# The causal triangle of an attention layer as zeros written after the exponential, in place of mask products

## The chip, the cores and the metric

The kernel runs on one core of one Trainium2 chip. The metric is device time in microseconds (us) of that core. PE is TensorE, DVE is VectorE, ACT is ScalarE, POOL is GpSimd, SP is the engine that here only issues DMAs.

## The reference

The computation is two rounds of a layer A and a layer B, each added to a residual `x` of 2048 tokens and width 512, with 32 heads of width 16. Layer A is a causal attention inside each of four segments of 512 tokens, mixed with a running memory:

```python
mask = (ar[:, None] < ar[None, :]) * -1000000000.0
for s in range(N):                       # N = 4 segments of L = 512
    logits = einsum('bhqd,bhkd->bhqk', qs, ks) * scale + mask
    p = softmax(logits)
    a_dot = einsum('bhqk,bhkd->bhqd', p, vs)
    ...                                  # a_mem from the memory M, z
    o = g * a_mem + (1.0 - g) * a_dot
    M = M + phi(ks)^T vs ; z = z + sum(phi(ks))
x = x + o @ wo
```

Layer B is a linear attention. Its keys pass through `softmax(pk)` and `softmax(-pk)` over the 16 features of a head, so each head and token needs the sum of 16 exponentials, twice:

```python
phi_k = concat([softmax(pk), softmax(-pk)])
kv = einsum('bhsf,bhsd->bhfd', phi_k, v) ; z = phi_k.sum(over tokens)
o = (phi_q @ kv) / (phi_q @ z + 1e-06)
x = x + o @ wo
```

## The kernel before, in words

Tokens lie in 16 tiles of 128; a segment is four of them. For each of the two rounds L the program goes through the four segments s: normalise, project to keys and queries per group g of eight heads (`a_proj`), attention in two halves i0 = 0 and 2 of the segment (`a_att`), the output projection, and then the keys of layer B for that segment (`b_keys`). After the fourth segment come the queries of layer B (`b_query`), and in round 0 the normalisation and projections for round 1 run among them.

**Attention.** TensorE is used as two row groups of 64 rows, so matmuls come in pairs that run side by side. In `a_proj`, VectorE makes four masked copies of the keys per group with `tensor_scalar` (label Km, L679, tile pQ, 128 in all), so that heads can be stacked along the contraction. In `a_att` the logits of a key tile wholly before the queries are one group of products (label S) and one exponential into a tile PT. For the diagonal there are two kinds of tile: PF (pool pF, three buffers, label Sf, twice for each group of each half, 128 in all, 896 columns exponentiated) and PE (pool pE, two buffers, label Sd, once, 64 in all, 768 columns). Both add the causal mask on TensorE, as a last pair of products `two` times `tri`, where `tri` holds -1e9 above the diagonal of a 64 by 64 block and `two` stacks two unit matrices: 128 columns for Sf and 256 for Sd. So the exponential on ScalarE (L351, a helper) already writes zeros in the triangle. The products P·V (label PV, L326 through another helper) then take P as weights and read PF, PE and PT directly from ScalarE.

**Layer B's keys.** For a pair of token tiles, ScalarE writes exp(k) and exp(-k), 1024 columns each; VectorE reduces each with one `tensor_reduce` over 16 features (label Zred, L945, 28 of 1024 columns and 8 of 512), then takes reciprocals (rZ) and scales the values (Vt).

**Other VectorE work that the prediction names.** xn normalises (L594, L598, 64 instructions), phmax and phadd (L634, L635, 48 each) build phi, nmul and nadd (L1043, L1049) are in `b_query`, oadd (L851) adds the memory's part to the attention, Kev, Qev, Vev and res are evacuations of TensorE's results that ScalarE or VectorE may do. GpSimd computes the reciprocal root of the normalisation (rstd, L585 and L587, 60 each), scales one weight matrix in setup (L530, four instructions) and clears buffers.

**What sets the order.** Each operation is entered in a graph with the engines that may run it, a planner's cost in ns for each, and a flag `port` on operations that the planner is told use a shared resource of VectorE and GpSimd. The planner itself is not in the program: its answer is a compressed table (`ORDER`) that `place` reads: a global order of all operations, the engine of each, and the buffer of each tile. `emit` turns that into one in-order list of instructions for each engine, with a semaphore wait wherever an operation needs another engine's result or a buffer that another still uses. An engine never passes an instruction that waits.

Of the kernel before, what the change touches and what calls it, by code (L numbers as in the profile page):

```python
# [16 lines left out]
D = 512  # L17
# [280 lines left out]
class Kernel:  # L298
# [97 lines left out]
    def alloc(self):  # L396
# [9 lines left out]
        self.two64 = sb("two64", [128, 2, 64], BF16)  # L406
        self.tri = sb("tri", [128, 64], BF16)
# [42 lines left out]
    def setup(self):  # L450
# [39 lines left out]
        for g in range(NG):  # L490
            for hf in range(2):
# [16 lines left out]
        v(lambda e: e.tensor_tensor(self.two64[:], self.ident[:, 0:64][:, None, :].to_broadcast([128, 2, 64]),  # L508
                                    self.ident[:, 64:128][:, None, :].to_broadcast([128, 2, 64]), ALU.add), 120, [R("ident")], [R("two64")])
        tw = self.T(self.p1, "fold")  # L510
        v(lambda e: e.memset(tw.t[:, 0:128], -1e9), 150, [], [tw], eng=P)
        v(lambda e: e.affine_select(tw.t[:, 0:128], tw.t[:, 0:128], [[-1, 128]], ALU.is_gt, 0.0, base=0, channel_multiplier=1), 250, [tw], [tw], eng=P)
        for hf in range(2):
            v(lambda e, hf=hf: e.tensor_copy(self.tri[64 * hf:64 * hf + 64, :], tw.t[64 * hf:64 * hf + 64, 64 * hf:64 * hf + 64]), 100,
              [tw], [R("tri", hf)])
# [142 lines left out]
    def a_proj(self, L, s):  # L658
# [7 lines left out]
        for g in range(NG):  # L666
# [11 lines left out]
            for sl in range(4):  # L678
                fn = lambda e, KM=KM, KT=KT, sl=sl: e.tensor_scalar(  # L679
                    KM.t[:, :, sl % 2, :, 64 * (sl // 2):64 * (sl // 2) + 64], KT.t[:].rearrange("p (j h k) -> p j h k", j=4, h=2),  # L680
                    self.m4[:, sl:sl + 1], None, op0=ALU.mult)
                self.g.op({"dve": (262.0, fn)}, [KT, R("m4")], [KM[sl]], label="Km", port=True)
# [85 lines left out]
    def a_att(self, L, s, i0):  # L768
# [7 lines left out]
        oT = self.oT[("a", L, s * 4 + i0)] = self.T(self.p2, "oT")  # L776
        two = lambda hf: self.two64[64 * hf:64 * hf + 64].rearrange("p a b -> p (a b)")
        tri = lambda hf, n: self.tri[64 * hf:64 * hf + 64, None, :].to_broadcast([64, n, 64])
        trir = [R("two64"), R("tri", 0), R("tri", 1)]
        for gg in range(2):  # L780
            PV = self.T(self.pD, "pv")
            for g in (2 * gg, 2 * gg + 1):
# [5 lines left out]
                for j in range(i0 + 1):  # L788
                    for p in range(2):
# [6 lines left out]
                        else:  # L796
                            P = PF[p] = self.T(self.pF, "PF")
                            self.mm(lambda S=S, j=j, p=p, key=key, qry=qry: [
                                (S.t[:, hf * 512 + 256 - 192 * x:hf * 512 + 512 - 256 * x], key(hf, j, p, x), qry(hf, 64 * x, 256 - 64 * x), x == 0, False)
                                for x in range(2) for hf in range(2)] + [  # L800
                                (S.t[:, hf * 512 + 64:hf * 512 + 448].rearrange("p (b c) -> p b c", b=2)[:, :, 0:64], two(hf), tri(hf, 2), False, True) for hf in range(2)],
                                [], rd + trir, [S], opens=[P], label="Sf", rows=64, dur=252)
# [4 lines left out]
                self.mm(lambda S=S, key=key, qry=qry: [  # L807
                    (S.t[:, hf * 512 + p * 192 + 64 * (1 - x):hf * 512 + p * 192 + 192 - 128 * x], key(hf, i0 + 1, p, x), qry(hf, 128 + 64 * x, 128 - 64 * x), p + x == 0, False)
                    for p in range(2) for x in range(2) for hf in range(2)] + [
                    (S.t[:, hf * 512:hf * 512 + 384].rearrange("p (a b) -> p a b", a=2)[:, :, 0:128], two(hf), tri(hf, 4), False, True) for hf in range(2)],  # L810
                    [], rd + trir, [S], opens=[PE], label="Sd", rows=64, dur=286)
# [110 lines left out]
    def b_keys(self, L, c, parts):  # L922
# [4 lines left out]
        for part in parts:  # L927
            Es, Vts = {}, {}
            units = [part[i:i + 2] for i in range(0, len(part), 2)]
            for u in units:  # L930
# [9 lines left out]
                for sgn in range(2):  # L940
# [3 lines left out]
                             ACT.Exp, 512 * n, [S[0], S[512]][:n], [E[sgn]], scale=1.0 - 2.0 * sgn, label="kexp")  # L944
                    fn = lambda e, sgn=sgn, eo=eo, Z=Z, n=n: e.tensor_reduce(Z.t[:, 0:64 * n].rearrange("p (k s h) -> p k s h", k=n, s=2)[:, :, sgn, :],  # L945
# [177 lines left out]
COPIED = {(L, t) for L in range(2) for t in range(16)}  # L1123
N_WARM = 26
# [17 lines left out]
yRioR}L^Vpezz889_oz(@EPZ{ZWTjjL%5J%#7+40h8VdWb9OJf6c&^Z+m7Dr!NUsU^LJ4)g|6;1hg`X)rs!h2)qCCtxa^hy^hUcBJLBf@;!QYDKl^DXpW{^o-I{7wS
ssC=1o5^fU@HP(x}&S*a)Wpk~yLn$rt-Oi$<~bffmPp4w7(+DvUIExv+h*o!h#Z`w#3s19wRP4t}hQ(byN2WT{AqwG|V^58|<PTS}bU0{dl2sNgQY!Xh!DL4kl;to1
WTWKjBqvtpdGtn~2NH6dpy~F`@hz8OrdPv9V1ofkn^oU;JM?6hu=q!E0yx4%oV>&#+reb^?LH(&54WcGAk_OXNDo<nR8jYo<RFx{wI2umna0m^h@>q?kQw1DF<LNRD
qwhGH&eKGiKtJ#bT_8rE@e5X>ulO4K&>MV<?{E@Lri%C;r_gIEOmC?Oy`gu61XPNOQfbOTFX<KKq*lB&|429K1HC7rT$G<~Q32{pQ>i|kqX_s7Kj1XFPB-W_O{Y7Qm
vWP!e3XX@5~mqdh-Ok7-j;u&KKwpCpuW5m_T#1T9;N2}c^ZC~2JtdDpFYzUl9ZVb=2>`Jt|&Wi$J6l~+){g<m1pA)`KSghpyE`9zS1lzOS5SqEh0l@QPUh+Os7~9o|
FgDY4(kl&^eZgXXJC~Jex<kc}kv(=iwdrcS^;(@tiz8&%itKPP{ws%#-mSG=dkS5)?ocsS4%gl_?)j&b#oDd;sst2Xe-Ps3ZYT!GlTh5DMVKcpx9ngLnw<$$Rl0yf<
IQm-A2>!iVxOw2H6hV|jT#ijU?M_#{4=kKqM*C=W--!;<EP6Sti6aXddC&%;w;9)Sw+BD^SX!OQZ9B)G#{@?yLkk3`e>bRL;X@XEY6FU`yFGb{?7WixmcUW%{dCHWL
ykyqj~`FcK;2lJ}D8n4d7@mV}P-@xbb*?c3P&%^RCJR*<4CvYE^ya2DkBk?(WE|1Kk@MwGsU&vSRMSKCT$=C2&d?jDYm++;0D__hfi_Lr!pCV%Ms60BK$ZPXDyb<5V
8}seFF5khM@TR;Tug{zDojf+5Dt7T{qB-BqgTxWOhsWSCc>~^%$K`SOUcQg-=fUDAPsoq)1N<P5#}n~$JU&0qLqw>!#t-r1`~*MAPw~V&0YA;p@U#2^zr+vo@a!VL%  # L1150
&+jP+!1g2E&h(*=I{9(evg0T*SSwT;?u=r9v}k66Fx(H<wxZ=K2yvR-}zmBlYinj_<jC>KjcsOGyZ{p;h#AZKlm~Eia+PC`3s&(zTq$Vad|?5kRr82p+q{FUZ#<0Wd
=z?2raA#E5e9yBD{zoA_^{yh$JG5C?cwuBj$;CVz!toGRpa4fruvJi|8Vz$Rabz%rdJ?CSr+&Vv$%ZmWUW4fru><ifl5wOfKSx)MBYvCenx;GLeWYa?0f*g~%n-irn
&`+$y$-wc?OmC$@_nV!cQyc8PQ%mDnu~%RKUkOe`wOBqF`YAXbQsqLN%GPRmpBj4UHh%Dgg@C?e0wvhtiPDtC%KVz1aB_KBn-v&b!0i7X<ISS_-Oyds+@EV7FtqO>?
K^NFIOm?$Iii?X7exFCy*0wRaFD9eiy;*zW&_KW=TfG8jjikzaLC?raXHDaU4B`S*7a<C{RDv8SCnyez;$jkDIye@}`s-m74Dr$*M;<4N;p2&Rif+#4ji^}q%xGIau
LbAB5DXNQVqPD0Zs>n;?vbZA3$t|M1EUb#C`eKk8tQv?CvaoC@hKb^8xM(Gsi4v-$9HK^up{l4Vrb@}%@{YVAPKq0{kvJvlh^FF@Xf95Ro8pYPC928_vaV<>&WhXOs
%Rqah{NKXI3kXUr?RwcEhecpVzR0xr>JSFx@;@DiB4jwny&83xALYuCXS01qNAuGM~RW*nz$>vi?XVRD5r+0xU!;(Cx@$^Vvx8e-^upkytpM#i2E|W>>&Dx=CZfwEZ
T{FqLLb*2C9;(vMQy@sPd|`s-i}zx1xfos%EHaYP6cE=BamLzN)TjsQ%);Xd!=yE~1xsCclclVuTv0V#!(Ri(oRg9HVBdvFd@`sUFH*Dvqovzlle(fdo}cg8VGIiud
xlY$=wj6>7g)s1~R>YP>q2)~eNNu3DqksR?SLx+m(Wy6V1Yp%$w}YMg4RK8S`gp-dnLh=HP=d?_A?B?=X(M)HgND%;Br@|%1mma3=Xg>0gls+Y2!s;@rCTB^4CC>yE
93gs*LQGAlMWk=akHkQp)Yc*Q5Qq9$RHAXa4ZPZ@XK($pH)F<&sJQiccXYow5Q|(m~`CL2^L29!KmHX5dwNZ^1yVV2{Ms8AjR86%^bx;$9R$*nZYAPR!7vj4Jr^9HH
;dNNOQgOLTbySsgClyXMlhGtstz;b;T}G01WuP1<zRMU=$jGv@YAucGr8>zfI!Ic%RqasQRfrDN+mzCYWMWxeYwgG+GQ13y_2eYcS-uuRMUib}Z)Ic+?dXU)g7#^nt  # L1160
&XH4>%%Hg2kE0KKnLq1>X<sH>g!YLkZPc#=%~8B>>}IBs=B7GrjM(Ws<u9%d@_Q3Bed+ILZp<Z)fx3eZj^O&EnQe|k_B~FSwt7oMRhk>Oc&QBbRX4MS>-67>Z-b_n6
# [67 lines left out]
```

## Time and profile before

| | |
|---|---|
| median of 3 runs | 483.2 us (482.02 to 483.73) |
| span of the profiled execution | 481.9 us |
| time of that execution beside its span | not listed; the runs' median is 1.3 us above the span |
| PE busy | 452.9 us (94%), 11582 matmuls |
| DVE busy | 438.3 us (91%), 920 instructions |
| ACT busy | 425.9 us (88%), 560 instructions |
| POOL busy | 63.8 us (13%), 145 instructions |
| mean granted TensorE clock | 0.988 |

Busy time is the time that at least one instruction of the engine is running, by the records; records of neighbours on one engine overlap a little, and those of matmuls a lot. A row of the groups view reads: line, engine, operation, output<-input by the program's names, shapes, count | busy us, mean ns of one | idle us of the engine just before them, and what ended it. A row by source line or tile gives least/median/greatest ns. A row of the timeline gives start us, us, engine, line, operation, names, shapes and how many neighbouring instructions are merged. A row of the waits gives who waited for whom: us in total, times, longest us. A row of the windows gives the stretch in us, its length, then busy us and count of PE, PEld (weight loads), DVE, ACT and POOL, then the granted clock, the DMA share and GB/s.

### The profile page before, as it was taken

The page shows a single profiled execution, that of the slowest core. Times are in us where ns is not written, and L with a number is a line of the kernel's source. Part 1 is how long each engine was busy: PE and PEld are TensorE (multiplying, and loading weights), DVE is VectorE, ACT ScalarE, POOL GpSimd, SP SyncE. Part 2 cuts the span into 40 slices and gives each one's busy share as a digit, 9 for nine tenths or more (in the row PEclk, how much of TensorE's full clock was granted, in tenths as well). Part 3 has the DMA queues.
Part 4 walks back from the last instruction along what each step waited for, and adds up shares of the span by engine and source line. Part 5 has one row for each costly group of instructions (what it writes and reads, how often), then busy time and mean ns, then how long its engine had stood idle before and what let it go on. Part 6 is the DMA issues. An engine that isn't in the chain of part 4 may idle for free.

```text
span 481.9 us, 25218 instructions
## 1 busy us (share of the span) xinstructions
PE 452.9 (94%) x11582; PEld 298.4 (62%) x11582; DVE 438.3 (91%) x920; ACT 425.9 (88%) x560; POOL 63.8 (13%) x145
## 2 busy tenths in 40 slices
PE   8798889999989999998999999999999999999895
PEld 3346665757767677666555677576667666666553
DVE  4998999899889999898999999999999897998883
ACT  2598999999989998578999999999999999776892
POOL 2801120101010110200231041020002020110000
PEclk9999999999999999998999999999999999999799
DMA  8735254350144212200225344432204403100256
GB/s 216 199 83 139 39 90 69 47 86 21 41 68 69 37 15 48 41 1 5 46 52 96 57 72 59 79 67 47 31 4 62 77 16 59 37 12 3 46 93 196
DMA packets 89451, 30.37 MB, mean 63 GB/s; under 512 B 76000, under 2 KB 89344, under 8 KB 89344
## 3 DMA queue, kind: packets, MB, share of 16 engines
q1 hardware_dynamic: 88992, 28.46, 32.1%
q8 instruction: 91, 1.49, 1.3%
q10 hardware_dynamic: 288, 0.26, 0.2%
q0 software_dynamic: 64, 0.02, 0.1%
q14 instruction: 16, 0.13, 0.1%
HBM read 6.32 MB, written 2.10 MB: 17 GB/s over the span
## 4 chain that ended last, share of the span: by engine, by line
PE 54%; DVE 20%; ACT 17%; DMA 3%; issue 2%; SPq 2%; POOL 1%; DVEq 0%
PE D L341 35%; PE D L326 18%; ACT p L351 9%; ACT pF L351 5%; DVE p L635 3%; DVE pQ L679 2%; DVE stats L577 2%; ACT pE L351 2%; SPq L364 2%; DVE p L360 1%; DMA X<-in_A_x_dram 1%; DVE p L598 1%; DVE pK L360 1%; DVE p L847 1%; DMA pX<-p 1%
## 5 line engine op out<-in xcount | busy, mean ns | idle before, releaser
L351 ACT ACTIVATE p<-D 128x1024 bf16<-128x1024 f32 (+1 forms) x276 | 251.5, 956 | 27.5 <-PE D L341 15.9
L351 ACT ACTIVATE pF<-D 128x896 bf16<-128x896 f32 x128 | 117.3, 938 | 2.7 <-PE D L326 2.0
L326 PE MATMUL D<-pK,pQ 64*128 64x256 bf16 (+3 forms) x1536 | 113.9, 243 | 6.1 <-DVE pQ L679 2.3
L326 PEld LDWEIGHTS D<-pK,pQ 64*128 64x128 bf16 x1536 | 54.9, 94 | 45.6 <-ACT p L351 5.8
L326 PE MATMUL D<-pV,pF 64*128 64x34 bf16 x1024 | 75.8, 176 | 1.7 <-ACT pE L351 0.5
L326 PE MATMUL D<-pW,pF 64*128 64x34 bf16 x1024 | 73.0, 176 | 0.5 <-issue 0.5
L585 POOL TENSOR_SCALAR rstd<-mv 128x1 f32<-128x1 f32 x60 | 18.6, 321 | 357.4 <-DVE mv L578 357.4
L341 PE MATMUL D<-pX,WA_k 64*128 64x512 bf16 x256 | 64.7, 376 | 0.7 <-DVE pX L360 0.7
L341 PE MATMUL D<-pX,WA_q 64*128 64x512 bf16 x256 | 64.7, 377 | 0.1
L326 PEld LDWEIGHTS D<-pV,pF 64*128 64x128 bf16 x1024 | 56.8, 93 | 5.3 <-issue 2.2
L326 PEld LDWEIGHTS D<-pW,pF 64*128 64x128 bf16 x1024 | 52.4, 93 | 1.3 <-issue 0.5
L351 ACT ACTIVATE pE<-D 128x768 bf16<-128x768 f32 x64 | 52.5, 830 | 0.8 <-PE D L326 0.4
L326 PE MATMUL D<-pV,p 64*128 64x34 bf16 x1024 | 52.2, 175 | 0.9 <-issue 0.6
L326 PE MATMUL D<-pW,p 64*128 64x34 bf16 x1024 | 51.1, 176 | 0.0
L326 PEld LDWEIGHTS D<-pV,p 64*128 64x128 bf16 x1024 | 46.7, 93 | 2.7 <-ACT p L351 0.5
L326 PE MATMUL D<-tri,two 64*128 64x128 bf16 (+1 forms) x384 | 46.2, 234 | 0.0
L326 PEld LDWEIGHTS D<-pW,p 64*128 64x128 bf16 x1024 | 45.1, 93 | 1.6
L577 DVE BATCH_NORM_STATS2 stats<-X 128x6 f32<-128x512 bf16 x64 | 42.7, 680 | 3.7 <-DMA X<-in_A_x_dram 3.4
L326 PE MATMUL D<-pV,pE 64*128 64x34 bf16 x512 | 45.0, 175 | 0.0
L679 DVE TENSOR_SCALAR pQ<-p,m 128x512 bf16<-128x512 bf16 x128 | 44.2, 366 | 0.1
L326 PE MATMUL D<-pW,pE 64*128 64x34 bf16 x512 | 42.7, 175 | 0.3 <-issue 0.3
L945 DVE TENSOR_REDUCE pS<-p 128x64 f32<-128x1024 bf16 (+1 forms) x36 | 38.6, 1084 | 1.3 <-ACT p L351 1.3
(118 smaller groups left out, 1001.5 us busy)
## 6 DMA issues: line engine op xcount, KB each, us to landing
pW<-pV SPq DMA_DIRECT2D x16, 136.0 KB, 2.8
out_dram<-X SPq DMA_DIRECT2D x7, 256.0 KB, 3.3
X<-in_A_x_dram SPq DMA_DIRECT2D x3, 512.0 KB, 6.4
pX<-in_B_wqkv_dram SPq DMA_DIRECT2D x3, 512.0 KB, 5.2
p<-p SPq DMA_TRANSPOSE x76, 2.6
pX<-p SPq DMA_TRANSPOSE x54, 3.3
WA_k<-in_A_wk_dram SPq DMA_DIRECT2D x2, 256.0 KB, 6.4
WA_q<-in_A_wq_dram SPq DMA_DIRECT2D x2, 256.0 KB, 8.0
```

The source lines that it names most:

```text
L326: ins = e.matmul(out_ap, lhsT, rhs, start=st, stop=sp, tile_position=(basep(lhsT), basep(out_ap)))
L341: ins = e.matmul(out_ap, lhsT[64 * hf:64 * hf + 64], rhs[64 * hf:64 * hf + 64], start=k == 0 and i == 0, stop=k == 1 and i == len(lists[hf ...
L351: return self.g.op({"act": (dur, lambda e: e.activation(out_ap(), in_ap(), func, scale=scale))}, reads, writes, opens, label=label)
L360: "dve": ((340 if fast else n / 0.96 + 65), lambda e: e.tensor_copy(out_ap(), in_ap()))}
L364: return self.g.op({"sp": (1200.0, lambda e: [e.dma_start(out_ap(), in_ap(), transpose=True)])}, reads, writes, opens, kind="d", lat=1450. ...
L577: v(lambda e: e.bn_stats(self.stats[:, t, :], self.X[:, t, :]), 602, [R("X", t)], [R("st", t)], label="bn")
L585: v(lambda e: e.tensor_scalar(rs, self.mv[:, t, 1:2], LN_EPS, None, op0=ALU.add), 170, [R("mv", t)], [R("rstd", t)], eng="pool", label="rstd")
L598: v(lambda e: e.tensor_scalar(xn.t[:], self.X[:, t, :], self.mv[:, t, 0:1], self.rstd[:, t:t + 1], op0=ALU.subtract, op1=ALU.mult), 300, [ ...
L635: v(lambda e: e.scalar_tensor_tensor(dst.t[:], e_.t[:], 1.0, dst.t[:], op0=ALU.min, op1=ALU.add), 335, [dst, e_], [dst], label="phadd", po ...
L679: fn = lambda e, KM=KM, KT=KT, sl=sl: e.tensor_scalar(KM.t[:, :, sl % 2, :, 64 * (sl // 2):64 * (sl // 2) + 64], KT.t[:].rearrange("p (j h ...
L847: v(lambda e, pvv=pvv, rden=rden, part=part: e.tensor_tensor(part(o).rearrange("p (a h d) -> p a h d", a=2, h=16), pvv()[:, :, :, 0:16], r ...
L945: fn = lambda e, sgn=sgn, eo=eo, Z=Z, n=n: e.tensor_reduce(Z.t[:, 0:64 * n].rearrange("p (k s h) -> p k s h", k=n, s=2)[:, :, sgn, :], eo( ...
```

## The change

**Triangle.** The 384 mask products and their constants `two` and `tri` go. After each exponential into PF and PE two instructions run in place on the two (PF) or four (PE) diagonal blocks of 64 by 64 per half, 256 columns of PF and 512 of PE: first, always on GpSimd, a minimum with 3e38 (label cutf or cutd), so that an exponential of an unmasked logit that overflowed is finite; then (cutfm, cutdm) either on GpSimd a product with a table of ones and zeros, or on VectorE a minimum with a table of 3e38 and zeros. P·V waits for the second. The two tables (`keep`) are built in setup.

**Key sums.** For the 28 reductions over 1024 columns, GpSimd first adds the two halves of each head's 16 features (512 sums in fp32, label zh), then halves of those (256 sums), and VectorE reduces the remaining four per head (label Zred4).

**Km.** The masked copies of the keys may now run on GpSimd too.

**The table.** A new order, new buffers, and the engine of each operation. Read out against the old one, it has 519 operations on POOL (141 before), 982 on DVE (920), 564 on ACT (561) and as many as before on PE and SP. By label:

| operation | before | after |
|---|---|---|
| Km | 128 DVE | 73 DVE, 55 POOL |
| cutf, cutd | none | 128 and 64, all POOL |
| cutfm | none | 65 DVE, 63 POOL |
| cutdm | none | 50 DVE, 14 POOL |
| zh | none | 56 POOL (28 of 512 sums, 28 of 256) |
| key reduction | 36 DVE | 8 DVE as before, 28 DVE of 256 columns |
| Kev, Qev, Vev on DVE | 23, 27, 13 | 26, 23, 12 (the others on ACT) |
| res on DVE | 29 | 31 |
| buffer clears in setup | 7 POOL | 3 POOL, 4 DVE |

```diff
-        self.two64 = sb("two64", [128, 2, 64], BF16)
-        self.tri = sb("tri", [128, 64], BF16)
+        self.keep = sb("keep", [128, 2, 64], BF16)
...
+        big = self.T(self.p1, "fold")
+        for k, top in enumerate((1.0, 3.0e38)):
+            v(lambda e, top=top: e.memset(big.t[:, 0:128], top), 150, [], [big], eng=P)
+            v(lambda e: e.affine_select(big.t[:, 0:128], big.t[:, 0:128], [[1, 128]], ALU.is_ge, 0.0, base=0, channel_multiplier=-1), 250, [big], [big], eng=P)
+            for hf in range(2):
+                v(lambda e, k=k, hf=hf: e.tensor_copy(self.keep[64 * hf:64 * hf + 64, k, :], big.t[64 * hf:64 * hf + 64, 64 * hf:64 * hf + 64]),
+                  150, [big], [R("keep", k, hf)])
...
-                self.g.op({"dve": (262.0, fn)}, [KT, R("m4")], [KM[sl]], label="Km", port=True)
+                self.g.op({"dve": (262.0, fn), "pool": (650.0, fn)}, [KT, R("m4")], [KM[sl]], label="Km", port=True)
...
+        diag = lambda P: P.t[:, :, 64:448].rearrange("p a (b c) -> p a b c", b=2)[:, :, :, 0:64]
+
+        def cut(P, ap, n, label):
+            k = lambda i: self.keep[:, i, None, None, :].to_broadcast([128, n // 128, 2, 64])
+
+            self.g.op({"pool": (2.08 * n, lambda e: e.tensor_scalar(ap(), ap(), 3.0e38, None, op0=ALU.min))}, [P], [P], label=label, port=True)
+            self.g.op({"pool": (2.08 * n, lambda e: e.tensor_tensor(ap(), ap(), k(0), ALU.mult)),
+                       "dve": (n / 1.92 + 65, lambda e: e.tensor_tensor(ap(), ap(), k(1), ALU.min))}, [P] + kept, [P], label=label + "m", port=True)
...
-                                for x in range(2) for hf in range(2)] + [
-                                (S.t[:, hf * 512 + 64:hf * 512 + 448].rearrange("p (b c) -> p b c", b=2)[:, :, 0:64], two(hf), tri(hf, 2), False, True) for hf in range(2)],
+                                for x in range(2) for hf in range(2)] + ([] if CUTF else [
...
+                            if CUTF:
+                              cut(P, lambda P=P: diag(P), 256, "cutf")
...
+                if CUTD:
+                  cut(PE, lambda PE=PE: PE.t[:, :, 64:192].rearrange("p a (b c) -> p a b c", b=2), 512, "cutd")
...
+                    if (L, c) in HALVED and n == 2:
+                        sc = self.T(self.p2, "zs")
...
+                        self.g.op({"pool": (1120.0, lambda e, e3=e3, s3=s3: e.tensor_tensor(s3(), e3()[:, :, 0:8], e3()[:, :, 8:16], ALU.add))},
+                                  [E[sgn]], [sc], label="zh")
+                        self.g.op({"pool": (600.0, lambda e, s3=s3: e.tensor_tensor(s3()[:, :, 0:4], s3()[:, :, 0:4], s3()[:, :, 4:8], ALU.add))},
+                                  [sc], [sc], label="zh")
+                        fn = lambda e, sgn=sgn, s3=s3, Z=Z, n=n: e.tensor_reduce(Z.t[:, 0:64 * n].rearrange("p (k s h) -> p k s h", k=n, s=2)[:, :, sgn, :],
+                                                                                s3().rearrange("p (k h) d -> p k h d", k=n)[:, :, :, 0:4], AX.X, ALU.add)
+                        v(fn, 332, [sc], [Z[sgn]], label="Zred4")
+                        continue
...
+CUTF, CUTD = True, True
+HALVED = {(L, c) for L in range(2) for c in range(4)}
...
-c-rlH1GFW}vTa60y4Ggfwr$(CZQHhO+qP}nw(ag$wYu*)=lb4<KmHrz)!wTzvnn%k=8PGUReP@_tTL;@;<M;1F{{d|vFfY_tI2Ay+N=(%%j&WEtO0At8nMQ#32Vxlv
+c-pmk1Ds^Z@^wZ=I<q;pZQHhO+qP}nwr$(CZ7gPXXXd+AJ-csb@pj+$f3K?hRwX0i#EFyl_OD|SMN*O)Bmqf5fD|T3Dv~0k5~)mzl6a&Fp`;WkP0Em}q$Wv7YLVKc4yj
```

The numbers beside the engines in these calls are the planner's costs, not measurements.

More of the change, by code (lines that the diff above doesn't have):

```diff
@@ L405, in alloc @@
         self.eps6 = sb("eps6", [128, 1], F32)
-        self.two64 = sb("two64", [128, 2, 64], BF16)
-        self.tri = sb("tri", [128, 64], BF16)
+        self.keep = sb("keep", [128, 2, 64], BF16)
+        if not CUTD:
+            self.two64 = sb("two64", [128, 2, 64], BF16)
+            self.tri = sb("tri", [128, 64], BF16)
         self.ones8 = sb("ones8", [128, 8], F32)
@@ L776, in a_att @@
         oT = self.oT[("a", L, s * 4 + i0)] = self.T(self.p2, "oT")
+        kept = [R("keep", k, hf) for k in range(2) for hf in range(2)]
+        diag = lambda P: P.t[:, :, 64:448].rearrange("p a (b c) -> p a b c", b=2)[:, :, :, 0:64]
[4 more added lines that the diff above has]
+                       "dve": (n / 1.92 + 65, lambda e: e.tensor_tensor(ap(), ap(), k(1), ALU.min))}, [P] + kept, [P], label=label + "m", port=True)
         two = lambda hf: self.two64[64 * hf:64 * hf + 64].rearrange("p a b -> p (a b)")
         tri = lambda hf, n: self.tri[64 * hf:64 * hf + 64, None, :].to_broadcast([64, n, 64])
-        trir = [R("two64"), R("tri", 0), R("tri", 1)]
+        trir = [] if CUTD else [R("two64"), R("tri", 0), R("tri", 1)]
         for gg in range(2):
@@ L807, in a_att @@
                 self.mm(lambda S=S, key=key, qry=qry: [
[L808 to L811, printed above, removed]
+                    (S.t[:, hf * 512 + p * 192 + 64 * (1 - x):hf * 512 + p * 192 + 192 - 128 * x], key(hf, i0 + 1, p, x), qry(hf, 128 + 64 * x, 128 - 64 * x),
+                     p + x == 0, CUTD and p + x == 2) for p in range(2) for x in range(2) for hf in range(2)] + ([] if CUTD else [
+                    (S.t[:, hf * 512:hf * 512 + 384].rearrange("p (a b) -> p a b", a=2)[:, :, 0:128], two(hf), tri(hf, 4), False, True) for hf in range(2)]),
+                    [], rd + trir, [S], opens=[PE], label="Sd", rows=64, dur=172 if CUTD else 278)
                 self.act(lambda PE=PE: PE.t[:, :, 64:256], lambda S=S: S.t[:, :].rearrange("p (a b) -> p a b", a=2)[:, :, 0:384].rearrange("p a (c e) -> p a c e", c=2),
                          ACT.Exp, 768, [S], [PE], scale=0.25, label="expd")
+                if CUTD:
+                  cut(PE, lambda PE=PE: PE.t[:, :, 64:192].rearrange("p a (b c) -> p a b c", b=2), 512, "cutd")
                 def pvmm(p, ii, PV=PV, g=g, PT=PT, PF=PF, PE=PE):
```

156 lines of the change are left out of this document (85 added, 71 removed).

## The prediction

> **What bounds the kernel now.** I read the head of the profile page first, then its chain of work that ended last.
>
> ```profile
> span 481.9 us, 25218 instructions
> PE 452.9 (94%) x11582; PEld 298.4 (62%) x11582; DVE 438.3 (91%) x920; ACT 425.9 (88%) x560; POOL 63.8 (13%) x145
> PE 54%; DVE 20%; ACT 17%; DMA 3%; issue 2%; SPq 2%; POOL 1%; DVEq 0%
> ```
>
> Three engines are nearly full, no single one carries the chain, and only GpSimd (POOL) is free. The window view, cut at the edges of the page's slices in which the attention products use pF (slices 3 to 16 and 21 to 35), says where:
>
> ```profile
> core 0: us, PE busy (x) PEld busy (x) DVE busy (x) ACT busy (x) POOL busy (x), PEclk, DMA share, GB/s
> 24.10:192.80 168.70, 159.59 (x4584) 110.42 (x4582) 157.36 (x320) 160.59 (x201) 18.04 (x40) 1.00 0.35 61
> 192.80:241.00 48.20, 45.60 (x946) 29.20 (x942) 43.24 (x99) 38.44 (x55) 6.41 (x16) 0.96 0.12 23
> 241.00:421.70 180.70, 175.88 (x4838) 118.53 (x4836) 171.83 (x366) 174.59 (x223) 24.74 (x52) 1.00 0.34 54
> 421.70:482.00 60.30, 52.53 (x1042) 31.14 (x1038) 48.21 (x94) 42.32 (x61) 1.58 (x4) 0.93 0.30 70
> ```
>
> Every edit but the setup and a few key sums acts in rows 1 and 3, together 349.4 us. There PE works 335.5, ScalarE 335.2, VectorE 329.2 (94%): VectorE stands idle only 20.2 us, GpSimd 306.6. So relief on one engine buys little, and anything that holds up VectorE by more than its small idle time is paid in full.
>
> **PE: the mask products go.** The timeline of PE around one mask pair of each size:
>
> ```profile
> 300.40 0.22 PE L326 MATMUL D<-tri,two 64*128 64x128 bf16 x2
> 300.46 0.18 PE L326 MATMUL D<-pV,p 64*128 64x34 bf16 x1
> ...
> 23.52 0.27 PE L326 MATMUL D<-tri,two 64*128 64x256 bf16 x2
> 23.63 0.38 PE L341 MATMUL D<-WA_v,pX 64*128 64x512 bf16 x2
> ```
>
> A pair runs on two row groups at once and holds PE from its start to the next start: 0.06 us for Sf, 0.11 us for Sd. 128 × 0.06 + 64 × 0.11 = 14.7 us of PE, not the 46 us that the summed durations suggest. This lies beside full VectorE and ScalarE, so alone I count it at nothing; it keeps PE (452.9 - 14.7 = 438) from being first in line.
>
> **VectorE: its own work.** Rows of the groups view, with shapes kept apart:
>
> ```profile
> L679 DVE TENSOR_SCALAR pQ<-p,m 128x512 bf16<-128x512 bf16 x128 | 44.2, 366 | 0.1
> L945 DVE TENSOR_REDUCE pS<-p 128x64 f32<-128x1024 bf16 x28 | 33.4, 1206 | 1.3 <-ACT p L351 1.3
> L945 DVE TENSOR_REDUCE pS<-p 128x32 f32<-128x512 bf16 x8 | 5.2, 658 | 0.0
> L1043 DVE TENSOR_TENSOR p<-p,pS 128x1024 bf16<-128x1024 bf16 x32 | 21.6, 685 | 1.8 <-ACT p L351 1.6
> L1049 DVE TENSOR_TENSOR p<-p 128x512 bf16<-128x512 bf16 x26 | 10.5, 418 | 0.3
> L360 DVE CAST p<-D 128x512 bf16<-128x512 f32 x27 | 18.5, 684 | 1.9 <-PE D L867 1.4 <-PE D L341 0.4
> L898 DVE TENSOR_TENSOR X<-X,D 128x1024 bf16<-128x1024 bf16 x23 | 27.9, 1216 | 4.1 <-PE D L341 3.7
> 28.01 0.87 DVE L679 TENSOR_SCALAR pQ<-p,m 128x512 bf16<-128x512 bf16 x3
> ```
>
> The last row is of the timeline: three key masks Km (0.347 us each) end after 0.87 us, so starts are 0.26 us apart and a record overlaps the next by 0.085 us, which I take off every added or removed instruction.
> Km, 55 moved to GpSimd: -55 × 0.26 = -14.4. Key sums: the reduction of 1024 takes 1.206, of 512 0.658; going on in the same step, 256 take 0.384 (estimate): -28 × 0.82 = -23.0. The second halves of the cut that the table puts on VectorE: a two-operand bf16 instruction takes 0.685 for 1024, 0.418 for 512, hence 0.284 for 256 (estimate): 65 × 0.20 + 50 × 0.333 = +29.6. If the broadcast table or the blocks of 64 denied it the rate of those rows, they would cost up to the cast's 0.684 for 512; that end would add 20, the lower end nothing. I take the two-operand rows, the same kind of instruction. Evacuations traded with ScalarE (Kev +3, Qev -4, Vev -1, residual +2, and single ones) net under 1 us by the cast's 0.684 and the residual's 1.216; setup is as small. Sum: **-8 us**.
>
> **ScalarE** has the same exponentials, and some 3 evacuations more: +1 to +2 us, in its 56 us of idle time. SP's queue and DMAs are untouched in number.
>
> **GpSimd: what it gets.** Its rows, by source line:
>
> ```profile
> L530 POOL TENSOR_TENSOR WA_v<-WA_v,gt x4: 1101/1103/1134, 16.3 to 19.6; 128x512 bf16<-128x512 bf16 x4
> L541 POOL MEMSET pF<- x3: 202/203/343, 20.6 to 20.9; 128x128 bf16 x3
> L539 POOL MEMSET pE<- x2: 304/456/607, 13.5 to 16.1; 128x256 bf16 x2
> L585 POOL TENSOR_SCALAR rstd<-mv x60: 202/221/1439, 11.1 to 424.0; 128x1 f32<-128x1 f32 x60
> ```
>
> Two operands: 1.10 us for 512, so 0.55 for 256 (estimate). 63 × 0.55 + 14 × 1.10 (cut on GpSimd) + 28 × (1.10 + 0.55) (key sums begun) = 96 us. One operand is in no row at these sizes. Lower bound a memset, which reads nothing: 0.304 for 256, by the step from 128 0.51 for 512; upper bound the two-operand row. 128 first halves of 256, 64 of 512 and 55 Km of 512: 99 to 201 us. No row is nearer to one end, so the middle, 150. GpSimd gets about **246 us (195 to 298)**, nearly all in the 349 us where it works 42.8 now: 83% there.
> The Trainium skill ("GPSIMD Engine Reference", Engine selection) says one-input work there runs roughly at line rate. That would be the low end, 195 us, and the forecast below would come out about 8 us lower; no run here shows it.
>
> **What GpSimd's work does to VectorE.** This is the term that decides. The one place where GpSimd already runs long instructions beside Km (timelines of both, one stretch, then the groups of that stretch):
>
> ```profile
> 16.35 4.33 POOL L530 TENSOR_TENSOR WA_v<-WA_v,gt 128x512 bf16<-128x512 bf16 x4
> ...
> 17.08 4.31 DVE L679 TENSOR_SCALAR pQ<-p,m 128x512 bf16<-128x512 bf16 x5
> ...
> L679 DVE TENSOR_SCALAR pQ<-p,m 128x512 bf16<-128x512 bf16 x5 | 4.3, 924 | 0.0
> ```
>
> Five Km that take 0.347 us elsewhere took 0.924 on average: each began and then stood until GpSimd's instruction was through. VectorE lost 5 × (0.924 - 0.347) = 2.9 us to 4.33 us of GpSimd, 0.67 us per us. It goes the other way too:
>
> ```profile
> 244.14 0.68 DVE L1043 TENSOR_TENSOR p<-p,pS 128x1024 bf16<-128x1024 bf16 x1
> 244.74 0.75 DVE L1049 TENSOR_TENSOR p<-p 128x512 bf16<-128x512 bf16 x2
> ...
> 244.14 1.44 POOL L585 TENSOR_SCALAR rstd<-mv 128x1 f32<-128x1 f32 x1 [4.14 <-DVE mv L578]
> ```
>
> A 0.22 us GpSimd instruction lasted 1.44 us while VectorE ran two-operand instructions. So two-operand bf16 work and fast one-operand work on SBUF exclude GpSimd. By the table, 438 of VectorE's 982 instructions will be of these kinds (Km 73, normalise 64, the phi pair 96, nmul and nadd 58, oadd 24, Vt 8, cut 115): 45%. If they met GpSimd at random the loss would be 0.45 × 0.67 = 0.30 us per us: 0.30 × 246 = 74 us.
> The same rule stands in the Trainium skill ("SBUF — State Buffer", Who interferes with whom): an exclusive lock, whoever starts first keeps it for the whole instruction, and VectorE's reductions are free of it. The rows agree on both directions; that reductions are free no row here shows.
> The bounds are 0 (the order keeps the two kinds apart) and 74. The calls flag just these instructions with port, so the order was laid out with them marked, but neither engine waits for the other's lock by a semaphore, and no row of before shows how far an order holds on the chip. I take half, **+37 us**. The 20 us that VectorE idles in these stretches may swallow some; it waits there mostly for PE and loads, so I take nothing off and let the range reach down.
>
> **The path of the exponentials.** P·V waited for ScalarE; now for one GpSimd instruction and a second on GpSimd or VectorE behind it: 0.43 + 0.28 to 0.55 us for pF, 0.80 + 0.42 to 1.10 for pE, plus lock waits.
>
> ```profile
> L351 ACT ACTIVATE pF<-D 128x896 bf16<-128x896 f32 x128 | 117.3, 938 | 2.7 <-PE D L326 2.0
> PEld D L326 <- ACT pF L351: 6.9, 25, 0.6
> ```
>
> In the old table's order, a mean of 5.5 ScalarE instructions stand between such an exponential and the first P·V that reads it, and 7.5 in the new one (pE 7.2 and 9.2). ScalarE runs 424 instructions in 349.4 us, 0.82 each, so the new order gives 1.6 us more: enough for 1.0 or 1.9 us on an idle GpSimd, little on a queue. I cost it at nothing. If that cover is gone, PE stands in order at P·V, and pF's three buffers (one new tile each 349.4 / 128 = 2.7 us, so 8.2 us of life) run out: ScalarE's exponential waits next.
>
> **The sum.** 481.9 - 8 + 37 = 510.9. The page gives the span alone; the median of the runs, 483.2, is 1.3 above it. Forecast **512 us**.
>
> **The rivals.** *A, faster:* the order holds and the lock costs little. VectorE loses its 8 us, PE its 15, ScalarE none: 481.9 - 8 + 1.3 = 475. For it: the port flags, and GpSimd's 306 idle us. Against: the five Km. It decides below 8 us of lock loss, 0.03 us per us of GpSimd, a twentieth of what the L530 stretch shows. *B, random meeting:* the full 74 us, 549. For it: two engines that free-run for 349 us; against: VectorE's non-excluding instructions (casts and residuals, 0.68 to 1.22 us) give GpSimd room to finish. *C, GpSimd itself becomes the bound:* at the upper durations it has 298 + 42.8 = 341 us of the 349, and the rstd instruction's mean of 0.321 us against its median of 0.221 says 0.1 us of lock wait for each instruction; 378 more such make 38, together 379. With the same 6% of stalls that VectorE has there, 402, or 53 us more than now: 481.9 + 53 + 1.3 = 536. The row for that mean:
>
> ```profile
> L585 POOL TENSOR_SCALAR rstd<-mv 128x1 f32<-128x1 f32 x60 | 18.6, 321 | 357.4 <-DVE mv L578 357.4
> ```
>
> Between the forecast and A lies no change: a loss of 6.5 to 9.5 us.
>
> **The numbers.** Half loss (490 to 530) 0.47; B and C, over 530, 0.24; A 0.25; within 0.3% (1.5 us, about what the spread of the runs can tell from nothing) 0.04. Slower 0.71, same 0.04, faster 0.25. The likeliest case's own range is 490 (20 idle us of VectorE swallow the lock) to 530; to hold 8 in 10 the range goes to A's 475 less a few us of PE's relief, 468, and to nearly B, 545.
>
> **What would show it.** PE near 438 us busy. Km, normalise, phadd and nmul on VectorE with a longer mean than now, Km most (0.35 to 0.5 or more), while casts and reductions keep theirs: the lock. VectorE's busy share up although its work shrank; if its busy time falls to 430, A is right. GpSimd's one-operand 256 between 0.30 and 0.55 us. PE's weight loads waiting for POOL or for the cut on VectorE by tens of us would be C. The prediction is wrong if the excluding instructions keep their durations.

## The result, and the profile after

The changed kernel takes 605.6 us (median of 4 runs, 604.9 to 606.2) against 483.5 for the kernel before: a ratio of 1.254, 95% interval 1.249 to 1.259. The forecast was 512 in a range of 468 to 545: right in sign, and far too small.

The head and the chain of the page after:

```profile
span 604.0 us, 24922 instructions
PE 486.6 (81%) x11198; PEld 294.3 (49%) x11198; DVE 499.9 (83%) x982; ACT 440.4 (73%) x563; POOL 468.3 (78%) x523
POOL 61%; PE 19%; ACT 8%; DVE 7%; issue 2%; DMA 2%; SPq 0%; POOLq 0%; ACTq 0%
POOL pF L793 15%; PE D L341 14%; POOL pQ L689 14%; POOL pE L793 13%; POOL pF L794 6%; ACT p L351 5%; PE D L326 4%; POOL rstd L597 3%; POOL p L973 3%; POOL pE L794 2%; POOL p L975 2%; ACT pF L351 2%; POOL rstd L595 1%; DMA X<-in_A_x_dram 1%; DVE pF L795 1%
```

GpSimd, with 1% of the chain before, now carries 61% of it. Its largest items there are the first halves of the cut (L793) and Km (L689), the one-operand instructions. The windows over the two attention stretches:

```profile
30.20:256.70 226.50, 178.35 (x4428) 107.68 (x4426) 191.29 (x348) 166.75 (x202) 210.18 (x227) 0.93 0.25 46
302.00:558.70 256.70, 204.72 (x4828) 126.24 (x4822) 212.34 (x415) 188.59 (x232) 230.03 (x248) 0.91 0.23 39
```

GpSimd is busy 440 of 483 us there (93% and 90%); no other engine passes 85%. From the first exponential into pF or pE to the last of the layer it was 165 us in each round before; now it is 227 and 220. These 117 us are nearly all of the added time.

The GpSimd rows, first as groups (busy us, mean ns), then by source line (least, median and greatest ns):

```profile
L793 POOL TENSOR_SCALAR pF<-pF 128x256 bf16<-128x256 bf16 x128 | 113.1, 888 | 11.5 <-ACT pF L351 11.2
L793 POOL TENSOR_SCALAR pE<-pE 128x512 bf16<-128x512 bf16 x64 | 99.2, 1552 | 3.8 <-ACT pE L351 3.6
L689 POOL TENSOR_SCALAR pQ<-p,m 128x512 bf16<-128x512 bf16 x55 | 92.6, 1688 | 7.6 <-ACT p L359 7.6
L794 POOL TENSOR_TENSOR pF<-pF,keep 128x256 bf16<-128x256 bf16 x63 | 44.6, 708 | 4.0
L973 POOL TENSOR_TENSOR p<-p 128x512 f32<-128x512 bf16 x28 | 33.6, 1200 | 3.2 <-ACT p L351 3.2
L975 POOL TENSOR_TENSOR p<-p 128x256 f32<-128x256 f32 x28 | 20.9, 750 | 0.9
L794 POOL TENSOR_TENSOR pE<-pE,keep 128x512 bf16<-128x512 bf16 x14 | 16.4, 1171 | 0.3
...
L793 POOL TENSOR_SCALAR pF<-pF x128: 836/850/1533, 31.0 to 533.1; 128x256 bf16<-128x256 bf16 x128
L793 POOL TENSOR_SCALAR pE<-pE x64: 1476/1499/2083, 28.5 to 523.5; 128x512 bf16<-128x512 bf16 x64
L794 POOL TENSOR_TENSOR pF<-pF,keep x63: 661/668/1132, 43.4 to 529.3; 128x256 bf16<-128x256 bf16 x63
```

On the same tile and shape the one-operand minimum takes 0.85 us where the two-operand product takes 0.67. The forecast had taken the two-operand price for an upper bound.

VectorE's groups, and three waits that were small or absent before (ScalarE's for PE at pF was 2.0 us):

```profile
L645 DVE SCALAR_TENSOR_TENSOR p<-p 128x512 bf16<-128x512 bf16 x48 | 39.9, 839 | 0.5
L689 DVE TENSOR_SCALAR pQ<-p,m 128x512 bf16<-128x512 bf16 x73 | 38.2, 534 | 3.4 <-ACT p L359 3.3
L608 DVE TENSOR_SCALAR p<-X,mv,rstd 128x512 bf16<-128x512 bf16 x48 | 26.4, 557 | 7.8 <-POOL rstd L597 7.6 <-POOL pQ L689 0.2
L871 DVE TENSOR_TENSOR p<-D,pS 128x512 bf16<-128x512 f32 x32 | 22.1, 690 | 0.9
L977 DVE TENSOR_REDUCE pS<-p 128x64 f32<-128x256 f32 x28 | 11.2, 406 | 3.3 <-POOL p L975 3.3
...
ACT pF L351 <- PE D L326: 50.5, 46, 5.0
PE D L326 <- POOL pF L794: 24.3, 20, 4.6
PEld D L326 <- POOL pQ L689: 16.3, 7, 4.3
```

Three of these groups in the kernel before, where the line numbers differ:

```profile
L635 DVE SCALAR_TENSOR_TENSOR p<-p 128x512 bf16<-128x512 bf16 x48 | 32.0, 674 | 0.2
L598 DVE TENSOR_SCALAR p<-X,mv,rstd 128x512 bf16<-128x512 bf16 x48 | 18.8, 402 | 1.4 <-POOL rstd L587 1.2
L847 DVE TENSOR_TENSOR p<-D,pS 128x512 bf16<-128x512 f32 x32 | 22.0, 688 | 0.8
```

The lock, VectorE held up by GpSimd, is plain: phadd went from 0.674 to 0.839, Km from 0.366 to 0.534, xn from 0.402 to 0.557, while an instruction that reads PSUM (L871, 0.688 before) kept its time. It depends on the form that GpSimd runs. A Km on VectorE beside a two-operand sum on GpSimd, and one beside a one-operand minimum (timelines):

```profile
105.91 1.15 POOL L973 TENSOR_TENSOR p<-p 128x512 f32<-128x512 bf16 x1
106.05 1.17 DVE L689 TENSOR_SCALAR pQ<-p,m 128x512 bf16<-128x512 bf16 x1
...
358.40 0.93 POOL L793 TENSOR_SCALAR pF<-pF 128x256 bf16<-128x256 bf16 x1
358.74 0.34 DVE L689 TENSOR_SCALAR pQ<-p,m 128x512 bf16<-128x512 bf16 x1
```

The first stood until GpSimd was through, the second ended inside GpSimd's instruction at its usual length. In this trace 35 VectorE instructions of the kinds that lengthened began inside a two-operand GpSimd instruction with room for their usual length and 0.1 us more, and one ended inside it; beside one-operand ones 96 of 105 did.

Below, "held" is the sum over VectorE's instructions of what each took beyond the median of its shape in the kernel before (for the cut, beyond the three that met no GpSimd work, 0.278 and 0.419 us): 62 us here. But it did not end the chain; VectorE's share fell from 91% to 83%, because PE and ScalarE stood waiting for GpSimd.

### The profile page after: what moved, and what is told of

The parts are those of the page before. It is cut to its first block, busy times and chain, and to the rows that moved or that the text cites. A ratio compares the mean times of both kernels' runs of the same rounds, so it can differ in the third digit from the quotient of the medians.

```text
span 604.0 us, 24922 instructions
## 1 busy us (share of the span) xinstructions
PE 486.6 (81%) x11198; PEld 294.3 (49%) x11198; DVE 499.9 (83%) x982; ACT 440.4 (73%) x563; POOL 468.3 (78%) x523
## 4 chain that ended last, share of the span: by engine, by line
POOL 61%; PE 19%; ACT 8%; DVE 7%; issue 2%; DMA 2%; SPq 0%; POOLq 0%; ACTq 0%
POOL pF L793 15%; PE D L341 14%; POOL pQ L689 14%; POOL pE L793 13%; POOL pF L794 6%; ACT p L351 5%; PE D L326 4%; POOL rstd L597 3%; POOL p L973 3%; POOL pE L794 2%; POOL p L975 2%; ACT pF L351 2%; POOL rstd L595 1%; DMA X<-in_A_x_dram 1%; DVE pF L795 1%
## 5 line engine op out<-in xcount | busy, mean ns | idle before, releaser
L351 ACT ACTIVATE pF<-D 128x896 bf16<-128x896 f32 x128 | 116.5, 921 | 51.4 <-PE D L326 50.5
L326 PE MATMUL D<-pK,pQ 64*128 64x256 bf16 (+3 forms) x1536 | 122.6, 261 | 31.8 <-POOL pQ L689 13.4
L793 POOL TENSOR_SCALAR pF<-pF 128x256 bf16<-128x256 bf16 x128 | 113.1, 888 | 11.5 <-ACT pF L351 11.2
L326 PE MATMUL D<-pV,pF 64*128 64x34 bf16 x1024 | 80.1, 179 | 39.6 <-POOL pF L794 15.5
L793 POOL TENSOR_SCALAR pE<-pE 128x512 bf16<-128x512 bf16 x64 | 99.2, 1552 | 3.8 <-ACT pE L351 3.6
L689 POOL TENSOR_SCALAR pQ<-p,m 128x512 bf16<-128x512 bf16 x55 | 92.6, 1688 | 7.6 <-ACT p L359 7.6
L326 PE MATMUL D<-pW,pF 64*128 64x34 bf16 x1024 | 77.7, 179 | 0.0
L341 PE MATMUL D<-pX,WA_k 64*128 64x512 bf16 x256 | 69.0, 394 | 0.5 <-ACT pF L351 0.5
L341 PE MATMUL D<-pX,WA_q 64*128 64x512 bf16 x256 | 69.1, 394 | 0.1
L794 POOL TENSOR_TENSOR pF<-pF,keep 128x256 bf16<-128x256 bf16 x63 | 44.6, 708 | 4.0
L795 DVE TENSOR_TENSOR pF<-pF,keep 128x256 bf16<-128x256 bf16 x65 | 31.4, 483 | 19.3 <-POOL pF L793 19.0
```

The source lines that it names most:

```text
L326: ins = e.matmul(out_ap, lhsT, rhs, start=st, stop=sp, tile_position=(basep(lhsT), basep(out_ap)))
L341: ins = e.matmul(out_ap, lhsT[64 * hf:64 * hf + 64], rhs[64 * hf:64 * hf + 64], start=k == 0 and i == 0, stop=k == 1 and i == len(lists[hf ...
L351: return self.g.op({"act": (dur, lambda e: e.activation(out_ap(), in_ap(), func, scale=scale))}, reads, writes, opens, label=label)
L689: fn = lambda e, KM=KM, KT=KT, sl=sl: e.tensor_scalar(KM.t[:, :, sl % 2, :, 64 * (sl // 2):64 * (sl // 2) + 64], KT.t[:].rearrange("p (j h ...
L793: self.g.op({"pool": (2.08 * n, lambda e: e.tensor_scalar(ap(), ap(), 3.0e38, None, op0=ALU.min))}, [P], [P], label=label, port=True)
L794: self.g.op({"pool": (2.08 * n, lambda e: e.tensor_tensor(ap(), ap(), k(0), ALU.mult)), "dve": (n / 1.92 + 65, lambda e: e.tensor_tensor(a ...
```

## The experiments

The variants keep the changed kernel's table, but for three at the places named, which are edits of the kernel before. Operations of given labels are left out after the table is read, and their dependencies passed on to whoever depended on them, or they are given another engine in the same place (line numbers shift with each edit):

```diff
+            o.eng = FORCE.get(o.label, o.eng)
...
+        gone = [o for o in order if o.label in DROP or (o.label, o.eng) in DROP]
```

Theory Q: the amount of work in GpSimd's in-order list decides. Theory L: the lock's cost to VectorE decides. Three more enter in the expectations: O (the new order itself costs the time), P (the added hops on the path from the exponential to the product) and V (VectorE is the bound as soon as GpSimd is not).

**Without the first halves** (`DROP = {"cutf", "cutd"}`)

> The changed kernel without the 192 first halves of the cut (the minimum with 3e38 on GpSimd); the second halves stay where they are, so an overflowed exponential would no longer be made finite. It takes 113.1 + 99.2 = 212 us of work from GpSimd and nothing from any other engine. Theory Q (GpSimd's in-order list is the bound in the attention stretches, 440 us of work in 483 us): the time falls until VectorE is next, whose 500 us of busy time lose about half of the 63 us that they stand at the lock: 500 to 530 us. Theory L (the lock's loss on VectorE sets the time, 63 us for some 404 us of added GpSimd work, 0.16 us per us): 605 - 0.16 x 212 = about 572 us.

Measured 525.3 us, and 43 us held on VectorE, 62 in the changed kernel. Q's range holds it; L is off by 47. Chain and busy time:

```profile
PE 460.9 (88%) x11198; PEld 286.9 (55%) x11198; DVE 476.7 (91%) x982; ACT 433.2 (83%) x563; POOL 265.8 (51%) x331
PE 36%; DVE 32%; ACT 19%; POOL 7%; DMA 3%; issue 3%; SPq 0%; DVEq 0%; ACTq 0%; POOLq 0%
```

**Km back on VectorE** (`FORCE = {"Km": "dve"}`)

> The changed kernel with all 128 Km on VectorE, in the same places of the order. It takes 92.6 us from GpSimd and gives VectorE 55 x 0.26 = 14 us of work, with some 14 us less of lock. Theory Q: 605 - 92.6 / 0.92 would be 504, but VectorE with 500 us of work is next, so 515 to 545. Theory L: VectorE's sum is unchanged, 595 to 610.

Measured 569.4, between the two. VectorE is busy 510.7 us (90%), 60 of them held, and the chain is shared by VectorE (34%) and GpSimd (27%). Taking 93 us from GpSimd saved 36: the two engines are tied together, and the next bound was nearer than Q had it.

**Triangle by products again** (cuts dropped, the mask products back, their tables built in the place of `keep`)

> The changed kernel with the triangle by mask products again and no cut; Km and the key sums stay shared with GpSimd, in the new order. GpSimd loses 273 us of work, VectorE 58 us and the larger part of its lock waits, PE gains 15. Theory Q: about 485 to 505, with GpSimd at 195 us. Theory L: 605 - 58 - 43 = 504. A third theory, O (the new order is bad by itself, since it was laid out for other durations): above 550.

Measured 518.2, outside all three ranges, with 12 us of PE at the start waiting for the tables, which this edit built late. Repeated with the tables built early:

> e_tri_back with the two mask tables built early, as in e_order: the new order with only Km and the key sums shared with GpSimd. e_tri_back was 518 with 12 us of PE waiting for the tables at the start. So 505 to 512: these two parts are worth 0 to 8 us against e_order's 513, since VectorE is relieved of 37 us and loses 18 at the lock, and other engines set the rest.

Measured 508.9, in the expected range.

**The order alone** (cuts and zh dropped, products and whole reductions back, Km on VectorE)

> Only the new order and its buffers are left: triangle by products, Km on VectorE, key sums in one reduction. Theories Q and L: 483 to 505, the price of an order that was laid out for other work. Theory O: above 550.

Measured 516.6, between the two ranges, with 7 us of the same late tables in it. With early tables:

> As e_all_back, with the two mask tables built right behind the unit matrix, so that PE does not wait for them at the first diagonal (7.4 us there). What is left is the order and the buffers alone: 505 to 512 us, 5% above the kernel before, since every place was laid out for other durations. If the order cost nothing in itself, 483 to 488.

Measured 513.3, 1 us above the range, and 1.065 times the kernel before (1.052 to 1.078): 31 us for the same work in the new order, with GpSimd only 12% busy. 513 is also above the 505 that Q and L allowed and far from O's 550: the order is a part, not the whole cause.

**First halves in the two-operand form**

```diff
-            self.g.op({"pool": (2.08 * n, lambda e: e.tensor_scalar(ap(), ap(), 3.0e38, None, op0=ALU.min))}, [P], [P], label=label, port=True)
+            self.g.op({"pool": (2.08 * n, lambda e: e.tensor_tensor(ap(), ap(), k(0), ALU.mult))}, [P] + kept, [P], label=label, port=True)
```

> The changed kernel with the first halves of the cut as a two-operand product with the table of ones and zeros on GpSimd in place of the one-operand minimum (an overflow would no longer be made finite; the second halves stay, though they change nothing any more). In the changed kernel the two-operand form takes 0.67 us for 256 and 1.15 for 512, the one-operand form 0.85 and 1.50: 128 x 0.18 + 64 x 0.35 = 45 us less on GpSimd, with the same number of instructions, waits and places. Theory Q (GpSimd's list is the bound): 605 - 45 / 0.92 = 556, so 550 to 565. Theory L (the lock): 605 - 0.16 x 45 = 598. A fourth theory, P (the two more hops on the path from the exponential to the product set the time, not GpSimd's sum): 590 to 605, since the hops stay.

Measured 595.2: Q missed, and L by 3 us, at a rate that the held time does not bear out. The profile says why. GpSimd's list did get shorter, by 33 us, but VectorE's held time rose from 62 to 99 us, and VectorE was busy 90%:

```profile
PE 482.0 (81%) x11198; PEld 294.0 (50%) x11198; DVE 533.9 (90%) x982; ACT 439.8 (74%) x563; POOL 435.0 (73%) x523
DVE 33%; POOL 30%; PE 23%; ACT 10%; issue 2%; DMA 2%; SPq 0%; DVEq 0%; POOLq 0%; ACTq 0%
L623 DVE TENSOR_SCALAR p<-X,mv,rstd 128x512 bf16<-128x512 bf16 x48 | 34.1, 716 | 4.3 <-POOL rstd L612 4.3
```

xn, 0.402 before and 0.557 in the changed kernel, takes 0.716. So on GpSimd the two forms differ twice: the one-operand form is longer, the two-operand form holds VectorE more. P's range holds 595 as well; the next pair tells P from Q.

**First halves short, hop kept** and **first halves long, hop gone**

```diff
+            one = lambda: P.t[:, 0:1, 64:65]
+            self.g.op({"pool": (2.08 * n, lambda e: e.tensor_scalar(one(), one(), 3.0e38, None, op0=ALU.min))}, [P], [P], label=label, port=True)
...
+            b = self.g.op({"pool": (2.08 * n, lambda e: e.tensor_scalar(scr, scr, 3.0e38, None, op0=ALU.min))}, [], [], label=label, port=True)
+            b.deps.add(self.g.ops[b.id - 1])
```

> The changed kernel with the first halves of the cut on a single column (the rest would no longer be made finite): every instruction, wait and place in the order stays, GpSimd's work falls by 128 x (0.88 - 0.22) + 64 x (1.55 - 0.22) = 170 us. Theory Q (how much GpSimd has to do in its order decides): near e_no_first's 525, so 525 to 545. Theory P (the extra hop from ScalarE to GpSimd and on, with its wait, decides): 575 to 605.

> The other half of that test: the first halves run on a scratch tile (256 columns for pF, 320 for pE, the few ahead of PE's last warm-up products left out, and nothing made finite), so they wait for the exponential as before, but no second half and no product waits for them. About 175 of the 212 us stay in GpSimd's list, the hop is gone from the path. Theory Q: the second halves and Km still stand behind them in GpSimd's list, 555 to 595. Theory P: the path is that of e_no_first, 525 to 540.

Measured 530.6 and 578.8, both in Q's ranges and outside P's. The hop by itself costs 5 us over e_no_first; the work (182 of the 212 us), though nothing reads its result, costs 54. Together that is 59 of the 80 us that the first halves cost; the other 21 are not split further. In the second run the waits show the rest of the list standing behind it:

```profile
L818 POOL TENSOR_SCALAR scr<-scr 128x256 bf16<-128x256 bf16 x128 | 114.9, 898 | 17.2 <-ACT pF L374 12.2 <-POOL scr L818 3.1 <-ACT pS L785 0.2
...
PE D L349 <- POOL pF L820: 29.3, 25, 4.4
PEld D L349 <- POOL pQ L713: 20.9, 10, 4.3
```

**A GpSimd load beside the kernel before**

```diff
+                b = self.g.op({"pool": (0, lambda e, ap=ap: e.tensor_scalar(ap, ap, 3.0e38, None, op0=ALU.min))}, [], [self.R("onesb")], label="load beside")
+                b.deps.add(x)
```

Here `x` is an exponential into pF or pE.

> The kernel before, unchanged in its work and order, with GpSimd given 256 one-operand minimum instructions of 256 columns on a scratch tile of its own, one behind each exponential into pF and two behind each into pE; nothing waits for them but GpSimd's own later work. It is the lock by itself: 256 x 0.85 = 218 us of GpSimd. Theory L: VectorE, 94% busy in the attention stretches, loses 0.16 to 0.30 us per us, 35 to 65 us, and the time is 515 to 545. Rival: VectorE's waits fall into its idle time or behind other engines, 483 to 495.

Measured 539.3 (ratio 1.119, 1.110 to 1.129), in the range of L, but not for L's reason. Only 12 us were held on VectorE:

```profile
L1111 POOL TENSOR_SCALAR scr<-scr 128x256 bf16<-128x256 bf16 x256 | 227.3, 888 | 126.7 <-ACT pF L355 70.1 <-ACT pE L355 34.9 <-POOL scr L1111 15.4
L640 DVE SCALAR_TENSOR_TENSOR p<-p 128x512 bf16<-128x512 bf16 x48 | 33.7, 708 | 0.2
...
POOL scr L1111 <- ACT pF L355: 70.1, 51, 5.3
DVE p L603 <- POOL rstd L592: 31.4, 15, 6.6
DVE nb L597 <- POOL rstd L592: 14.3, 6, 4.6
```

VectorE waited 46 us in two rows for rstd, which stood in GpSimd's list behind instructions that waited for a ScalarE exponential. Nothing but GpSimd's own later work waits for the load, yet that order made a path of it. So this run prices the one-operand lock at 12 / 227 = 0.05 us per us, and shows a second way in which a long GpSimd list costs time; it does not measure the lock alone.

**Only the second halves** and **no first halves, Km back**

> Of the change only the second halves of the cut are left (115 on VectorE, 77 on GpSimd), in the new order; no first halves, Km and key sums back. Against e_order (513) it takes 15 us from PE, gives VectorE 30 us of work, GpSimd 62 us of two-operand work, and VectorE 0.3 x 62 = 18 us at the lock. VectorE then has 443 + 30 + 18 = 491: theory V (VectorE is the bound as soon as GpSimd is not): 525 to 540. If VectorE's work does not matter in this order: 505 to 515.

> e_no_first with all Km on VectorE as well: GpSimd keeps some 175 us (the cut's second halves there, the key sums, rstd). Theory Q, with GpSimd no longer the bound in e_no_first (51% busy, 7% of the chain): about the same as e_no_first, 512 to 528, VectorE being next. Theory L: the lock's loss falls by 0.16 x 93 = 15 us and VectorE's own work rises by 14, 520 to 530.

The first measured 536.3, as V expected, with 18 us held for 62 us of two-operand work on GpSimd: 0.30 us per us. The second measured 533.1, outside both ranges and 8 us above e_no_first. That Km is better on GpSimd once GpSimd is not the bound is one reading. But in both runs GpSimd waits 12 to 13 us at the start for the `keep` table, whose copies now stand behind Km on VectorE; how much of the 8 us that is stays open.

**The cut alone in the old order** (the old table, Km and key sums as before; each first half behind its exponential, each second half ten places on or ahead of its first reader)

> The order and buffers of the kernel before, with the cut in place of the mask products: each first half right behind its exponential in the old order, each second half ten places on or just ahead of its first reader (about half of pF's and a fifth of pE's on GpSimd, the others on VectorE); Km and key sums as before. GpSimd has 212 us of first halves, some 60 of second halves and 55 of rstd. The new order alone costs 31 us on the old work (e_order). If it earns that back by its later products (7.5 instead of 5.5 exponentials between), the old order is worse with the cut than e_km_back (569, which has the key sums besides): 575 to 610. If it earns nothing, about 569 - 31: 530 to 550.

Measured 675.5, outside both ranges, with GpSimd only 49% busy and 33 us held. Everyone waits in turn:

```profile
POOL pF L820 <- ACT pF L383: 161.3, 74, 6.4
ACT pF L383 <- PE D L358: 87.0, 59, 5.6
PEld D L358 <- POOL pF L821: 42.9, 25, 4.4
DVE pF L822 <- POOL pF L820: 37.8, 26, 4.6
```

The waits fit theory P after all, in an order that leaves no room: exponential, GpSimd, second half, product, and back to a buffer for the next exponential. The new order, which cost 31 us in e_order, carries the cut far better: e_km_back, with the key sums besides, took 569. The places of the cut's instructions here are simple ones, so 675 is what this placement costs, not the best of the old order.

**One Km in four on GpSimd, in the kernel before** (`"pool" if sl == 3 and L + s > 0 else "dve"`)

> The kernel before in its own order with one in four Km on GpSimd (28 of 128, none in the first segment) and nothing else changed. VectorE is relieved of 28 x 0.26 = 7 us and loses by the one-operand rate of e_beside, 0.05 us per us, 28 x 1.6 x 0.05 = 2 us. By its sums alone the time would be 478 to 483. If the longer instruction is what counts (1.6 us in place of 0.35, PE waiting for all four Km of a group in order, and rstd behind it in GpSimd's list), 488 to 510.

Measured 487.3, ratio 1.008 (0.9995 to 1.016): no gain; it lies between the two expectations, and its interval touches no change. VectorE was held 6 us for 47 us of Km on GpSimd, 0.14 us per us and not the 0.05 of the expectation. No variant beat the kernel before.

## Why the prediction was wrong, by its steps

In steps from the kernel before, each the difference of two medians: the order alone +31 (e_order), Km and key sums shared -4 (e_tri_back2, not clear of noise), second halves for products +16 (e_no_first), first halves +80 (the changed kernel). Each step starts where the one before ended, so that they add up to about the 122 us measured shows nothing by itself, and in another sequence a step could be worth something else.

- **GpSimd's price failed, and most of the miss hangs on it.** "One operand is in no row at these sizes ... upper bound the two-operand row": the true price lay above that bound's 201 us: 305 us (113.1 + 99.2 + 92.6) in place of 150. The bound was an assumption on two kinds of instruction that no row related. The sentence on the Trainium skill there ("GPSIMD Engine Reference", Engine selection: one-input work roughly at line rate) leaned further in the wrong direction: from 256 to 512 the minimum grows by 2.5 ns per element, the product by 1.9. The planner's own costs in the change (532 and 1065 ns for the minimum, 650 for Km) make 172 us of the same work; an order laid out with measured prices was not run.
- **"This is the term that decides" failed too: the lock was not what ended last.** Put into the forecast's own sum, the true price would have given 0.15 x (96 + 305) = 60 us in place of 37, about 535.
- **Rival C was the right mechanism and got the smaller chance.** With 341 us in its list it gave 536; with the measured 440, the same sum (440 x 1.06 - 349 = 117 us more) gives about 600. e_no_first, e_short_first and e_first_aside show GpSimd's list as the bound from three sides. VectorE stands close behind it: in e_km_back and e_two_operand, 86 and 33 us less busy time on GpSimd saved 36 and 10 us.
- **The lock.** For two-operand work the random-meeting rate, 0.30, was right: e_no_first_km_sums gives 0.30, e_two_operand 0.30 to 0.33 (99 held, less 5 to 13 for Km at the one-operand rates, for 291 us). "I take half" was not: nothing kept the two kinds apart. For one-operand work the rate is small, 0.05 in e_beside and 0.14 in e_old_order_km, and 96 of 105 VectorE instructions ended inside such an instruction. So the rule of the Trainium skill ("SBUF — State Buffer", Who interferes with whom) that whoever issues first holds the shared ports for the whole instruction does not describe that form here; beside the two-operand form the trace agrees with it, 34 of 35. Two errors met: 62 us were held, between the 37 taken and the bound of 74.
- **"I cost it at nothing" (the path)** had the cover named rightly, "enough ... on an idle GpSimd, little on a queue", and the queue came. PE's waits for the cut, and ScalarE's 50.5 us for PE before pF, are what the text listed as next.
- **A term was missing: the order itself.** The table was counted for what it moves, not for what its other places cost work that kept VectorE 94% busy in the old one: 31 us.
- **Right:** VectorE's own work (Zred4 0.406 us against 0.384, the cut 0.278 and 0.419 in three undisturbed ones, 0.288 and 0.412 in 42 of e_old_order_cut, against 0.284 and 0.418); casts and PSUM readers untouched; Km at 0.53. **Wrong:** "PE near 438 us busy". It rose to 486.6: in a slower, more broken run PE's records are longer (L341 from 0.377 to 0.394 us, granted clock 0.988 to 0.917) and overlap less.

## What to carry to other kernels

An idle engine is not a free one: price its instructions by rows of the same form, and where there is no row, leave the upper end open instead of borrowing another form's. Then add up its list inside the stretch where the work falls, not over the whole span, and ask what else stands behind each waiting instruction in it. An order laid out by hand or by a planner is part of the price of every change: run the new order with the old work once, and the two can be told apart.

## What the runs showed of the hardware that was not expected

- GpSimd's one-operand bf16 instruction is slower than its two-operand one: 0.85 against 0.67 us for 256 columns, 1.50 against 1.15 for 512, and from its start to the next one's, where that followed at once, 0.825 against 0.635 and 1.469 against 1.129; Km, with a per-partition scalar, 1.58 (medians undisturbed or nearly so).
- The one-operand form costs VectorE less per us: 0.05 to 0.14 against about 0.30, and 96 of 105 VectorE instructions with room to end beside it did, against 1 of 35.
- The granted TensorE clock fell with PE's share: 0.988 in the kernel before (PE 94% busy), 0.973 in e_order (91%), 0.917 after (81%), 0.856 in e_old_order_cut (75%). No run here separates it from the waits that came with it.
